# Scores computed with the keys on the partitions and row sums by a product with ones, in an attention block followed by a SoLU feed-forward

## The chip, the cores and the metric

The kernel runs on one NeuronCore of a Trainium2 chip. The metric is the device time of one execution in microseconds (us); smaller is better. The engines are named as in the profile: PE (matrix products and transposes; PEld is its weight load), DVE (vector engine), ACT (activation engine), POOL (GpSimd) and SP, which here only issues the input transfers.

## What is computed

The reference, cut to what matters. Eight batches, twelve heads, 448 positions, head size 64; then 3584 tokens of 768 features through a feed-forward of width 1024.

```
q_n, k_n = rmsnorm(q, g_q), rmsnorm(k, g_k)       # over the 64 values of a head
scores = matmul(q_n, k_n^T) / sqrt(64)
attn = exp(scores - max(scores)) ; attn /= sum(attn) + 1e-9
x = concat over heads of matmul(attn, v)          # 3584 x 768
h = x @ w_in ; e = exp(h - max(h)) ; solu = h * e / (sum(e) + 1e-9)
ln = (solu - mean) / sqrt(var + 1e-6) * g_ln
out = ln @ w_out                                  # w_in, w_out are float64 in memory
```

Everything on the chip is float32. The two weight matrices arrive as 64-bit floats and are taken apart into float32 by integer operations.

## The kernel before

A **pair** is two heads of one batch; there are 48 pairs, six to a batch. For pair n the kernel does, in this order:

- `load`: q and k of both heads by one transfer each, and v, on SP's queue, three pairs ahead.
- `norm` (L136 to L152), one pair ahead: squares on ACT, sums on DVE, the power -1/2 on POOL, then q scaled on DVE and k scaled on POOL.
- `qk_transpose` (L165, L170): eight transposes on PE into two PSUM tiles `pt`; DVE copies both out with the gains as a factor, to `qkT`.
- `scores` (L180 to L186), for each quarter j of the query rows: two products on PE (one a head) put 112 queries on the partitions and 448 keys along the row, in `s`. DVE takes the row maximum (`nmax`), ACT makes the exponentials `E` and their row sums.
- `normalise` (L192 to L195): DVE inverts the eight sums, POOL multiplies all of `E` by them, two instructions of 112x1792.
- `e_transpose` (L206, L209), a pair later: 32 transposes on PE turn `E` round, so that the keys are on the partitions; DVE and ACT copy the four results out of PSUM as `ET`.
- `values` (L221, L227): eight products on PE, summed over the keys in `o`; DVE copies `o` to `xT`, the feed-forward's input.

The **feed-forward** works on tiles of 128 tokens, 28 in all, three or four to a batch. The first part of a tile is `ff_in` (L243, product `h`) and `ff_solu` (mostly DVE); the second is `ff_transpose` (`pu`) and `ff_out` (`po`, L286). The tiles of batch b-1 are cut in pieces and strewn between the pieces of the pairs of batch b; the last batch's four tiles follow alone.

The **weights** are converted in 28 steps during batch 0 (`load_w`, `convert_w`, L102 to L114): six or seven instructions on DVE, one on ACT, for `w_in` one on POOL.

The tile framework gives buffers in turn, adds the waits, and moves instructions of an engine against the order of the code; each engine then runs its own list strictly in order.

Of the kernel before, what the change touches and what calls it, by code (L numbers as in the profile page):

```python
# [9 lines left out]
FP32 = mybir.dt.float32  # L10
U32 = mybir.dt.uint32
I32 = mybir.dt.int32
AX = mybir.AxisListType.X
AF = mybir.ActivationFunctionType
OP = AluOpType


@with_exitstack
def kernel(
    ctx: ExitStack,  # L20
    tc: tile.TileContext,
    q: bass.AP,
# [95 lines left out]
    st = {}  # L118
# [92 lines left out]
    def values(n):


        b, hp = divmod(n, NP)
        d = st[n]
        if b // 2 not in xTs:
            xTs[b // 2] = work.tile([P, KD, 2 * S], FP32, tag="xT", name="xT")
        o = ps_t.tile([P, S], FP32, tag="t", name="o")
        for kc in range(NJ):
            for h in range(2):  # L220
                nc.tensor.matmul(  # L221
                    o[h * D : (h + 1) * D, :], d["v"][:, h, kc * D : (kc + 1) * D], d["ET", h][:, kc],
                    start=(kc == 0), stop=(kc == NJ - 1),
                )

        c0 = (b % 2) * S
        nc.vector.tensor_copy(  # L227
            xTs[b // 2][:, hp, c0 : c0 + S].rearrange("d (p j) -> d j p", j=NJ),
            o.rearrange("d (j p) -> d j p", j=NJ),
        )  # L230
        del st[n]

# [161 lines left out]
```

## Time and profile before

| | |
|---|---|
| median of three runs | 1436.75 us (1434.79 to 1441.49) |
| the profiled execution: its own time | 1442.7 us |
| its span, first to last instruction | 1440.9 us |
| granted TensorE clock, mean over the span | 0.937 of full speed |
| busy: PE, DVE, POOL, ACT | 1246.6, 803.3, 548.6, 482.0 us |

The span is cut below at the moments at which `xT` of a batch's last pair is written (batch 0 ends at 214 us, batch 1 at 378 us, batch 7 at 1349 us; what follows is the last four tiles). In these stretches PE and DVE change places: DVE is busier in the first, PE in all others. In "x16" and the like the profile counts two records for each product of the program, since a float32 product runs as two.

### The profile page before, as it was taken

What the parts mean: (1) busy time and instruction counts of PE and PEld (TensorE: products, weight loads), DVE (VectorE), ACT (ScalarE), POOL (GpSimd) and SP (SyncE); (2) the same over time, 40 slices, a digit from 0 to 9 for tenths busy, and PEclk for the clock granted to TensorE, in tenths of its full rate; (3) what the DMA queues carried; (4) which work ended last, traced back from release to release, by engine and by line L of the source; (5) the groups of instructions that cost most, each with busy time, mean ns of one, the idle gap of its engine ahead of it and who ended that gap; (6) DMA issues with size and microseconds to landing.
All of it is one profiled execution on the core that took longest, in us unless ns stands there. A gap on an engine that the chain in (4) does not pass through costs nothing.

```text
span 1440.9 us, 14104 instructions
## 1 busy us (share of the span) xinstructions
PE 1246.6 (87%) x5249; PEld 630.5 (44%) x5249; DVE 803.3 (56%) x1234; ACT 482.0 (33%) x1177; POOL 548.6 (38%) x239
## 2 busy tenths in 40 slices
PE   3466558899899998899899998899899998999998
PEld 1133224445444454444444454444444454445454
DVE  6889996554565445635564455736554454535331
ACT  3234232333333234234423334324323333324111
POOL 5662447325433253433433253343433243231100
PEclk9667678999999999999999999999999999999999
DMA  4322310101101010010100111011101001000000
GB/s 148 106 85 73 92 56 30 33 30 31 50 20 31 30 50 30 26 43 31 50 20 30 31 37 43 25 44 31 41 28 31 31 30 37 7 18 12 11 14 31
DMA packets 42717, 57.55 MB, mean 40 GB/s; under 512 B 3216, under 2 KB 35480, under 8 KB 42648
## 3 DMA queue, kind: packets, MB, share of 16 engines
q1 hardware_dynamic: 38592, 45.62, 10.8%
q10 hardware_dynamic: 4056, 11.02, 2.0%
q8 instruction: 42, 0.69, 0.2%
q14 instruction: 27, 0.22, 0.1%
HBM read 45.62 MB, written 11.01 MB: 39 GB/s over the span
## 4 chain that ended last, share of the span: by engine, by line
PE 44%; DVE 23%; POOL 12%; DMA 8%; issue 6%; ACT 6%; SPq 1%; ACTq 0%; POOLq 0%; DVEq 0%
PE po L286 15%; PE h L243 14%; POOL E L195 8%; DMA qk<-in_k_dram 7%; PE o L221 6%; PE s L180 5%; DVE nmax L184 5%; PE pe L206 4%; ACT E L186 3%; DVE rs L138 2%; DVE qkn L152 2%; POOL rs L144 2%; DVE qkT L170 2%; POOL qkn L152 2%; ACT sq L136 2%
## 5 line engine op out<-in xcount | busy, mean ns | idle before, releaser
L195 POOL TENSOR_TENSOR E<-E,sum 112x1792 f32<-112x1792 f32 x96 | 309.7, 3247 | 234.6 <-DVE sum L193 233.3
L243 PE MATMUL h<-w_in,xT 128*128 128x512 f32 x672 | 317.3, 622 | 19.6 <-ACT E L186 19.6
L286 PE MATMUL po<-w_out,uT 128*128 128x384 f32 x896 | 306.8, 495 | 14.0 <-ACT ET L209 8.6
L186 ACT ACTIVATE E<-s,nmax 112x448 f32<-112x448 f32 x384 | 240.6, 633 | 200.5 <-DVE nmax L184 198.5
L184 DVE TENSOR_REDUCE nmax<-s 112x2 f32<-112x896 f32 x192 | 207.5, 1083 | 140.4 <-PE s L180 140.2
L180 PE MATMUL s<-qkT 64*112 64x448 f32 x768 | 213.5, 634 | 75.7 <-DVE qkT L170 35.1
L144 POOL TENSOR_TENSOR rs<-rs,mhalf 112x16 f32<-112x16 f32 x48 | 142.7, 2974 | 269.2 <-DVE rs L143 269.2
L206 PE MATMUL pe<-ident,E 112*112 112x112 f32 x1536 | 200.8, 277 | 43.2 <-POOL E L195 40.8
L206 PEld LDWEIGHTS pe<-ident,E 112*112 112x112 f32 x1536 | 161.0, 141 | 163.8 <-issue 88.6
L286 PEld LDWEIGHTS po<-w_out,uT 128*128 128x128 f32 x896 | 167.9, 193 | 133.8 <-issue 14.2
L243 PEld LDWEIGHTS h<-w_in,xT 128*128 128x128 f32 x672 | 128.1, 198 | 177.3 <-issue 154.3
L221 PE MATMUL o<-ET,v 112*64 112x448 f32 x768 | 173.1, 558 | 16.2 <-DVE ET L209 15.8
L136 ACT ACTIVATE sq<-qk 112x1024 f32<-112x1024 f32 x48 | 50.8, 1058 | 325.5 <-DMA qk<-in_k_dram 292.6
L209 DVE COPY ET<-pe 112x448 f32<-112x448 f32 x192 | 117.9, 615 | 59.6 <-PE pe L206 59.0
L209 ACT COPY ET<-pe 112x448 f32<-112x448 f32 x192 | 100.4, 532 | 123.2 <-PE pe L206 119.8
L138 DVE TENSOR_REDUCE rs<-sq 112x16 f32<-112x1024 f32 x48 | 58.4, 1217 | 133.5 <-ACT sq L136 133.5
L180 PEld LDWEIGHTS s<-qkT 64*112 64x112 f32 x768 | 59.9, 186 | 159.6 <-issue 69.4
L266 POOL TENSOR_TENSOR he<-he,mhalf 128x1 f32<-128x1 f32 x28 | 15.4, 550 | 299.8 <-DVE he L265 299.8
L227 DVE COPY xT<-o 128x448 f32<-128x448 f32 x48 | 46.5, 968 | 98.5 <-PE o L221 98.2
L252 DVE TENSOR_REDUCE hmax<-h 128x1 f32<-128x1024 f32 x28 | 34.3, 1225 | 114.8 <-PE h L243 114.5
L221 PEld LDWEIGHTS o<-ET,v 112*64 112x64 f32 x768 | 53.6, 138 | 98.6 <-issue 73.2
L287 ACT COPY y<-po 128x384 f32<-128x384 f32 x56 | 26.7, 476 | 172.1 <-PE po L286 172.1
(43 smaller groups left out, 784.0 us busy)
## 6 DMA issues: line engine op xcount, KB each, us to landing
qk<-in_q_dram SPq DMA_DIRECT2D x48, 224.0 KB, 2.9
qk<-in_k_dram SPq DMA_DIRECT2D x48, 224.0 KB, 3.3
v<-in_v_dram SPq DMA_DIRECT2D x48, 224.0 KB, 2.6
out_dram<-y ACTq DMA_DIRECT2D x28, 384.0 KB, 2.3
raw<-in_moe_w_in_dram SPq DMA_DIRECT2D x12, 512.0 KB, 3.9
raw<-in_moe_w_out_dram SPq DMA_DIRECT2D x16, 384.0 KB, 3.2
grow<-in_g_q_dram ACTq DMA_DIRECT2D x2, 0.2 KB
grow<-in_g_k_dram ACTq DMA_DIRECT2D x2, 0.2 KB
```

What stands on the lines that cost most here:

```text
L136: nc.scalar.activation(sq, d["qk"], AF.Square)
L138: nc.vector.tensor_reduce(rs.rearrange("p s h j -> p (s h j)"), sq.rearrange("p s h (j d) -> p (s h j) d", d=D), AX, OP.add,)
L144: nc.gpsimd.tensor_tensor(rs.rearrange("p s h j -> p (s h j)"), rs.rearrange("p s h j -> p (s h j)"), mhalf[0:SP].to_broadcast([SP, 4 * NJ ...
L180: nc.tensor.matmul(s[:, h, 0:S], d["qkT"][hh, 0, j * SP : (j + 1) * SP], d["qkT"][hh, 1, :], start=True, stop=True)
L184: nc.vector.tensor_reduce(nmax, s[:, :, 0:S], AX, OP.max, negate=True)
L186: nc.scalar.activation(d["E"][:, h, j], s[:, h, 0:S], AF.Exp, bias=nmax[:, h : h + 1], accum_out=d["sum"][:, h, j : j + 1])
L195: nc.gpsimd.tensor_tensor(d["E"][:, h], d["E"][:, h], d["sum"][:, h].rearrange("p j -> p j ()").to_broadcast([SP, NJ, S]), OP.mult)
L206: nc.tensor.transpose(pt[:, j * SP : (j + 1) * SP], d["E"][:, h, j, kc * SP : (kc + 1) * SP], ident[0:SP, 0:SP])
L209: (nc.vector.tensor_copy if kc % 2 else nc.scalar.copy)(d["ET", h][:, kc], pt)
L221: nc.tensor.matmul(o[h * D : (h + 1) * D, :], d["v"][:, h, kc * D : (kc + 1) * D], d["ET", h][:, kc], start=(kc == 0), stop=(kc == NJ - 1),)
L243: nc.tensor.matmul(d["h"][:, hs], xTs[m][:, c, t * P : (t + 1) * P], w_in[:, c, hs], start=(c == 0), stop=(c == KD - 1))
L286: nc.tensor.matmul(po, d["uT"][:, c], w_out[:, c, hs], start=(c == 0), stop=(c == KF - 1))
```

## The change

The kernel's body becomes `general_path` (with small edits) and is put behind a branch on a flag: the largest |g_q * g_k| against 80/8 = 10. With the inputs of the reference the largest is 5.26, so the branch is not entered. A new `fast_path` runs first:

- `scores` gives the products the other way round, 112 keys on the partitions and 448 queries along the row, each head in a PSUM tile of its own. k is transposed raw, its norm factor enters as the exponential's per-partition scale, and both gains and 1/8 go into q's copy. No maximum is subtracted. `E` is then what `values` needs: no transposes of `E`, no copies, no maximum.
- Row sums: POOL adds the four key blocks (1792, then 896 elements) to `es`; PE multiplies `es` with a matrix of ones (`sm`), which gives the sum on 64 partitions for each head; DVE takes the reciprocal of 128x448 and multiplies `o` by it while copying to `xT`.
- q and k are loaded by one transfer a head (four a pair, pieces of 256 bytes; before: two a pair, pieces of 1024 bytes).
- The weights: `w_in` is converted in batch 0, `w_out` in batch 1. The second part of a tile lags by three tiles, so batch 1 has three first parts and no second part, and the end has four first and seven second parts.
- PSUM: one `h` tile of two banks, and six one-bank tiles that everything else shares (before: two two-bank tiles shared by `s` and `h`, four others).

```diff
+    def norm(n):
+        nc.scalar.activation(sq, d["qk"].rearrange("p s j h d -> p (s j h) d"), AF.Square)
+        nc.vector.tensor_reduce(flat, sq, AX, OP.add)
+        nc.vector.tensor_scalar(rs, rs, 1.0 / D, 1e-6, OP.mult, OP.add)
+        nc.gpsimd.tensor_tensor(flat, flat, mhalf[0:SP].to_broadcast([SP, 4 * NJ]), OP.pow)
+        nc.gpsimd.tensor_tensor(
+            d["qn"],
+            d["qk"][:, 0].rearrange("p j h d -> p (j h) d"),
+            rs[:, 0].rearrange("p j h -> p (j h) ()").to_broadcast([SP, NJ * 2, D]),
+            OP.mult,
+        )
...
+    def scores(n, kc):
...
+        for h in range(2):
+            hh = slice(h * D, (h + 1) * D)
+            s = d["s", h] = ps_t.tile([SP, S], FP32, tag="t", name="s")
+            nc.tensor.matmul(
+                s, d["qkT"][hh, 1, kc * SP : (kc + 1) * SP], d["qkT"][hh, 0, :], start=True, stop=True
+            )
+        for h in range(2):
+            nc.scalar.activation(d["E"][:, kc, h], d["s", h], AF.Exp, scale=d["rs"][:, 1, kc, h : h + 1])
+        if kc == NJ - 1:
+            es = d["es"] = work.tile([SP, 2, 2, S], FP32, tag="es", name="es", bufs=1)
+            nc.gpsimd.tensor_tensor(es, d["E"][:, 0:2], d["E"][:, 2:4], OP.add)
+            nc.gpsimd.tensor_tensor(es[:, 0], es[:, 0], es[:, 1], OP.add)
...
+    def values(n):
...
+        sm = ps_t.tile([P, S], FP32, tag="t", name="sm")
+        for h in range(2):
+            nc.tensor.matmul(sm[h * D : (h + 1) * D, :], ones[0:SP, :], d["es"][:, 0, h], start=True, stop=True)
+        r = work.tile([P, S], FP32, tag="r", name="r")
+        nc.vector.reciprocal(r, sm)
...
+        nc.vector.tensor_tensor(
+            xTs[b // 2][:, hp, c0 : c0 + S].rearrange("d (p j) -> d j p", j=NJ),
+            o.rearrange("d (j p) -> d j p", j=NJ),
+            r.rearrange("d (j p) -> d j p", j=NJ),
+            OP.mult,
+        )
...
+    LAG = 3
...
+            if len(waiting) > (LAG if b < B - 1 else 1):
+                fill += second(waiting.pop(0))
...
+    fast_path(tc, q, k, v, moe_w_in, moe_w_out, out, grow, within)
+    large = nc.values_load(flag[0:1, 0:1], min_val=0, max_val=1)
+    with tc.If(large > 0):
+        general_path(tc, q, k, v, g_q, g_k, moe_w_in, moe_w_out, moe_g_ln, out)
```

How the rows stand on the engines, first PE in a middle batch, where pairs and tiles are mixed. Before, from one `o` to the next transposed scores (`pe` is the transpose of `E`):

```order
L221 MATMUL o<-ET,v 64x448 x8
L165 MATMUL pt<-ident,qkn 128x112 x8
L243 MATMUL h<-w_in,xT 128x512 x6
L180 MATMUL s<-qkT 112x448 x2
L206 MATMUL pe<-ident,E 112x112 x16
L243 MATMUL h<-w_in,xT 128x512 x2
L180 MATMUL s<-qkT 112x448 x2
```

The `pe` rows stand between the scores, 32 of them to a pair. Now, PE in a middle batch:

```order
L607 MATMUL po<-w_out,uT 128x384 x8
L534 MATMUL o<-E,v 64x448 x8
L540 MATMUL sm<-es,ones 64x448 x2
L514 MATMUL s<-qkT 112x448 x2
L607 MATMUL po<-w_out,uT 128x384 x8
L514 MATMUL s<-qkT 112x448 x2
L501 MATMUL pt<-ident,qn 128x112 x4
L501 MATMUL pt<-ident,qk 128x112 x4
L564 MATMUL h<-w_in,xT 128x512 x6
L514 MATMUL s<-qkT 112x448 x4
```

The `pe` rows are gone; two `sm` products, which read POOL's `es`, have come in right behind `o`.

DVE in batch 0, before (`tmp` belongs to the weight conversion):

```order
L107 TENSOR_SCALAR tmp<-tmp 128x512
L184 TENSOR_REDUCE nmax<-s 112x2
L108 TENSOR_SCALAR tmp<-tmp 128x512
L209 COPY ET<-pe 112x448
L109 SCALAR_TENSOR_TENSOR tmp<-raw,tmp 128x512
L102 TENSOR_SCALAR tmp<-raw 128x512
L105 TENSOR_SCALAR tmp<-raw 128x512
L227 COPY xT<-o 128x4x112
```

And DVE in batch 0 now:

```order
L482 TENSOR_REDUCE rs<-sq 112x16
L483 TENSOR_SCALAR rs<-rs 112x16
L444 TENSOR_SCALAR tmp<-raw 128x512
L542 RECIPROCAL r<-sm 128x448
L446 SCALAR_TENSOR_TENSOR tmp<-raw,tmp 128x512
L545 TENSOR_TENSOR xT<-o,r 128x4x112
L505 TENSOR_SCALAR qkT<-pt,gcol 128x448
L447 TENSOR_SCALAR tmp<-raw 128x512
```

The maxima and the `ET` copies are gone from between the conversion's instructions, and one wide reciprocal a pair has come in. POOL in batch 0 now, one pair:

```order
L453 TENSOR_TENSOR w_in<-tmp 128x512 x2
L484 TENSOR_TENSOR rs<-rs,mhalf 112x16
L487 TENSOR_TENSOR qn<-qk,rs 112x512
L521 TENSOR_TENSOR es<-E 112x1792
L522 TENSOR_TENSOR es<-es 112x896
```

The two `E` instructions of 112x1792 have given way to two additions, of 112x1792 and 112x896.

## Rows read from the trace of the kernel before

**Rows 1.** Page, part 1: busy time, share of the span, instructions.

```profile
PE 1246.6 (87%) x5249; PEld 630.5 (44%) x5249; DVE 803.3 (56%) x1234; ACT 482.0 (33%) x1177; POOL 548.6 (38%) x239
```

**Rows 2.** Stretches: length, PE, PEld, DVE, ACT, POOL busy; clock, DMA share, GB/s.

```profile
core 0 of [0], span 1440.9 us
...
0.00:214.00 214.00, 116.65 (x465) 54.30 (x465) 186.05 (x299) 75.95 (x176) 105.58 (x49) 0.72 0.31 94
214.00:378.00 164.00, 146.08 (x616) 73.41 (x617) 87.80 (x132) 57.52 (x142) 73.89 (x32) 0.94 0.11 34
...
879.00:1036.00 157.00, 141.64 (x624) 71.64 (x624) 84.97 (x126) 56.70 (x141) 64.20 (x28) 0.97 0.11 34
1036.00:1210.00 174.00, 160.38 (x688) 81.99 (x688) 89.80 (x136) 59.30 (x146) 64.91 (x29) 0.98 0.11 33
1210.00:1349.00 139.00, 133.67 (x605) 68.81 (x602) 66.95 (x104) 46.24 (x119) 42.64 (x18) 0.99 0.04 14
1349.00:1441.00 92.00, 86.60 (x256) 45.65 (x256) 23.34 (x41) 11.00 (x20) 2.17 (x4) 1.00 0.05 18
```

**Rows 3.** Order of time, batch 0: start, duration, engine, line, operation.

```profile
46.99 0.68 DVE L104 SCALAR_TENSOR_TENSOR tmp<-raw,tmp 128x512 f32<-128x512 uint32 x1
47.59 0.41 DVE L107 TENSOR_SCALAR tmp<-tmp 128x512 int32<-128x512 int32 x1
47.93 1.08 DVE L184 TENSOR_REDUCE nmax<-s 112x2 f32<-112x896 f32 x1
...
127.68 6.62 POOL L195 TENSOR_TENSOR E<-E,sum 112x1792 f32<-112x1792 f32 x2 [19.31 <-DVE sum L193]
127.93 3.33 DVE L105 TENSOR_SCALAR tmp<-raw 128x384 uint32<-128x384 uint32 x1
```

**Rows 4.** Order of time, PE in middle and late batches at full clock.

```profile
703.05 0.98 PE L206 MATMUL pe<-ident,E 112*112 112x112 f32 x8
703.96 1.01 PE L180 MATMUL s<-qkT 64*112 64x448 f32 x4
705.81 3.23 PE L221 MATMUL o<-ET,v 112*64 112x448 f32 x16
...
1403.07 9.60 PE L243 MATMUL h<-w_in,xT 128*128 128x512 f32 x22
...
1425.94 10.59 PE L286 MATMUL po<-w_out,uT 128*128 128x384 f32 x32 [0.69 <-ACT uT L277]
```

**Rows 5.** Waits of PE: us in total, times, longest.

```profile
PE pe L206 <- POOL E L195: 40.8, 15, 9.0
PE s L180 <- DVE qkT L170: 35.1, 11, 5.5
```

**Rows 6.** Groups by line: busy us, mean ns of one | idle before.

```profile
L209 DVE COPY ET<-pe 112x448 f32<-112x448 f32 x192 | 117.9, 615 | 59.6 <-PE pe L206 59.0
L170 DVE TENSOR_SCALAR qkT<-pt,gcol 128x448 f32<-128x448 f32 x96 | 60.9, 665 | 8.9 <-PE pt L165 8.9
L138 DVE TENSOR_REDUCE rs<-sq 112x16 f32<-112x1024 f32 x48 | 58.4, 1217 | 133.5 <-ACT sq L136 133.5
L227 DVE COPY xT<-o 128x448 f32<-128x448 f32 x48 | 46.5, 968 | 98.5 <-PE o L221 98.2
```

**Rows 7.** Single lines: duration in ns, min/median/max.

```profile
L195 POOL TENSOR_TENSOR E<-E,sum x96: 3167/3175/5157, 29.8 to 1339.3; 112x1792 f32<-112x1792 f32 x96
...
L111 POOL TENSOR_TENSOR w_in<-tmp x12: 1258/1324/2314, 22.7 to 103.5; 128x512 f32<-128x512 f32 x12
...
L152 POOL TENSOR_TENSOR qkn<-qk,rs x48: 1037/1061/2487, 11.5 to 1269.4; 112x512 f32<-112x512 f32 x48
...
L193 DVE RECIPROCAL sum<-sum x48: 187/203/204, 28.6 to 1335.8; 112x8 f32<-112x8 f32 x48
...
L192 DVE TENSOR_SCALAR sum<-sum x48: 118/172/174, 28.2 to 1335.6; 112x8 f32<-112x8 f32 x48
```

**Rows 8.** Page, part 3: the input queue's packets, MB, share of 16 engines.

```profile
q1 hardware_dynamic: 38592, 45.62, 10.8%
```

More of the change, by code (lines that the diff above doesn't have):

```diff
@@ L18, with general_path @@
 @with_exitstack
-def kernel(
+def general_path(
     ctx: ExitStack,
@@ L201, in e_transpose @@
         if half == 0:
-            d["ET", h] = work.tile([SP, NJ, S], FP32, tag="ET", name="ET", bufs=3)
+            d["ET", h] = work.tile([SP, NJ, S], FP32, tag="ET", name="ET")
         for kc in (2 * half, 2 * half + 1):
@@ L209, in e_transpose, with values @@
             (nc.vector.tensor_copy if kc % 2 else nc.scalar.copy)(d["ET", h][:, kc], pt)
-    def values(n):
+    def values(n, h):
         b, hp = divmod(n, NP)
@@ L217, in values @@
             xTs[b // 2] = work.tile([P, KD, 2 * S], FP32, tag="xT", name="xT")
-        o = ps_t.tile([P, S], FP32, tag="t", name="o")
+        if h == 0:
+            d["o"] = ps_t.tile([P, S], FP32, tag="t", name="o")
         for kc in range(NJ):
[L220 to L231, printed above, removed]
+            nc.tensor.matmul(
+                d["o"][h * D : (h + 1) * D, :], d["v"][:, h, kc * D : (kc + 1) * D], d["ET", h][:, kc],
+                start=(kc == 0), stop=(kc == NJ - 1),
+            )
+        if h == 1:
+            c0 = (b % 2) * S
+            nc.vector.tensor_copy(
+                xTs[b // 2][:, hp, c0 : c0 + S].rearrange("d (p j) -> d j p", j=NJ),
+                d["o"].rearrange("d (j p) -> d j p", j=NJ),
+            )
+            del st[n]
     mt = {}
@@ L319, in pair @@
                 pieces.append(lambda h=h, half=half: e_transpose(n - 1, h, half))
-                if j == NJ - 1:
-                    pieces.append(lambda: values(n - 1))
+                if half:
+                    pieces.append(lambda h=h: values(n - 1, h))
             if j == 1 and n + 3 < B * NP:
@@ new lines, with kernel @@
+@with_exitstack
+def kernel(
+    ctx: ExitStack,
+    tc: tile.TileContext,
+    q: bass.AP,
+    k: bass.AP,
+    v: bass.AP,
+    g_q: bass.AP,
+    g_k: bass.AP,
+    moe_w_in: bass.AP,
+    moe_w_out: bass.AP,
+    moe_g_ln: bass.AP,
+    out: bass.AP,
+):
+    nc = tc.nc
+    D = q.shape[3]
+    P = 128
+    KF = moe_w_in.shape[1] // P
+    gains = ctx.enter_context(tc.tile_pool(name="gains", bufs=1))
+    grow = gains.tile([KF + 2, P], FP32, name="grow")
+    gg = gains.tile([P, 2, D], FP32, name="gg")
+    gmax = gains.tile([P, 1], FP32, name="gmax")
+    within = gains.tile([P, 1], FP32, name="within")
+    flag = gains.tile([1, 1], I32, name="flag")
+    nc.scalar.dma_start(grow[0:KF, :], moe_g_ln.rearrange("(c p) -> c p", p=P))
+    for i, g in enumerate((g_q, g_k)):
+        for h in range(2):
+            nc.scalar.dma_start(grow[KF + i : KF + i + 1, h * D : (h + 1) * D], g.rearrange("(o d) -> o d", o=1))
+    for i, g in enumerate((g_q, g_k)):
+        nc.scalar.dma_start(gg[:, i], g.rearrange("(o d) -> o d", o=1).to_broadcast([P, D]))
+    nc.vector.tensor_tensor(gg[:, 0], gg[:, 0], gg[:, 1], OP.mult)
+    nc.vector.tensor_reduce(gmax, gg[:, 0], AX, OP.max, apply_absolute_value=True)
+    nc.vector.tensor_scalar(flag, gmax[0:1], 80.0 / float(D) ** 0.5, None, OP.is_gt)
+    nc.vector.tensor_scalar(within, gmax, 80.0 / float(D) ** 0.5, float(D) ** -0.5, OP.is_le, OP.mult)
+    fast_path(tc, q, k, v, moe_w_in, moe_w_out, out, grow, within)
+    large = nc.values_load(flag[0:1, 0:1], min_val=0, max_val=1)
+    with tc.If(large > 0):
+        general_path(tc, q, k, v, g_q, g_k, moe_w_in, moe_w_out, moe_g_ln, out)
```

244 lines of the change are left out of this document (243 added, 1 removed).

## The prediction

> **What bounds the kernel now.** The page's busy times come first: PE is busy 87% of the span, everything else 56% or less [rows 1]. That is an average over stages, so I cut the span at the ends of the batches [rows 2]. The reader is to see three kernels in one. In batch 0 (0 to 214 us) DVE is busy 186 of 214 us and PE only 117, at a granted clock of 0.72: DVE sets the pace, because the weight conversion lies on it. In batches 1 to 7 PE is busy 134 to 160 us of 139 to 174 at a clock of 0.94 to 0.99: PE sets the pace, with some 14 us of idle time in a middle batch. In the last 92 us PE is busy 87 of them. So I ask of each edit: what does it take from DVE in the front, from PE behind it, and what comes in.
>
> DVE in the front has a second load that the busy time hides. The order of time shows a weight instruction (L105) of 3.33 us that starts while POOL multiplies `E` and ends with that POOL instruction [rows 3]; the instructions shown above it in that group follow each other every 0.34 and 0.60 us. DVE was standing behind POOL: part of its busy time is such waiting.
>
> **PE, batches 2 to 7.** Unit prices at full clock [rows 4]: eight transposes 0.98 us, two score products 1.01 us for one quarter (a pair has four), the eight products of `o` 3.2 us, `h` of a tile 9.60 x 24/22 = 10.5 us, `po` 10.6 us, `pu` (eight transposes) 1.0 us. A pair now costs 1.0 (`pt`) + 4.0 + 3.2 + 3.9 (32 transposes `pe`) = 12.1 us, a tile 22.1 us. Check: six pairs and four tiles make 161 us, and a four-tile batch shows 160.4 us busy [rows 2]; with three tiles 139 against 141.6. The change takes out the 3.9 us and puts in `sm`, two products of the shape of the eight in `o`: a quarter of 3.2, 0.8 us. A pair then costs 9.0 us, a batch 6 x 9.0 + 4 x 22.1 = 142 or 54 + 66 = 120 us. Three of each make 788 us.
>
> To this comes idle time. Now it is 15.4 and 13.6 us in the two middle batches shown and 5.3 in the last [rows 2]. The wait of `pe` for POOL's multiplied `E`, 40.8 us in all or 5.1 a batch, goes with `pe` [rows 5]. The wait of scores for `qkT`, 35.1 us, stays in kind: two copies still follow `pt`, only one of them goes to ACT. The maximum is no longer between a score and its exponential, which should free PSUM sooner; against it stands the new wait of `sm` for `es`. I let these two cancel and take 14.5 - 5.1 = 9.4 us for five batches, 5 for the last: 52 us. Batches 2 to 7: 840 us, now 971.
>
> `sm` costs no wait if `es` is there in time. Behind the last exponential of a pair POOL needs about 6 us (below); until `sm` PE has `pt` (1.0), two quarters of scores (2.0), `o` (3.2) and, in most pairs, a feed-forward piece of 1 to 5 us. That cover is thin: it is gone where no piece lies between or POOL is still at the next pair's norm, and then `sm` waits and the next scores queue behind it.
>
> **DVE, batches 0 and 1.** A conversion step is four instructions of 0.34 and two of 0.60 us [rows 3], 2.56 us; I take the same for `w_out`, which is narrower and has one more. Now six pairs share 28 steps, 11.9 us a pair. The attention's own DVE work is four maxima (4.3), `rs` (1.2), two `qkT` (1.3), four `ET` (2.5), `xT` (1.0) [rows 3, 6], the sums (0.4) [rows 7], about 1.0 for the small ones and q's scaling (an estimate): 11.7. Together 23.6 us a pair; shown are 186/6 = 31.0 [rows 2]. The missing 7.4 us are the standing behind POOL. POOL's streaming instructions make two `E` (6.3), k's scaling (1.1) and two weight products (2.5) a pair [rows 7], 9.9 us, so three quarters of POOL's streaming time is lost on DVE.
>
> The change puts a wide reciprocal on DVE. The trace has it only for 8 elements: 203 ns against 172 ns for an addition of the same tile [rows 7], 3.9 ns an element more. A copy of 448 elements out of PSUM takes 0.615 us [rows 6], 1.4 ns an element; together 5.3 ns or 2.4 us. Bounds: 0.6 us, if the 31 ns are a fixed cost, and 4.8 us, if all above the shortest addition (203 - 118 ns) grows with the elements. I take 2.4 us, since the difference of two equal tiles is the nearest thing to a price per element. It isn't on PE's path later, where DVE has half its time free, but it is in the front. The Trainium skill (VectorE: DVE Perf Modes, the section on the fixed hardware budget) says that a reciprocal is an iterated division with a repeat count of 8; if that meant eight passes an element at the 0.96 GHz of its overview page (Trainium Kernel Development and Optimization, NeuronCore Architecture), it would take 3.7 us, an estimate, and the sum would be 18 us higher. No row here shows a wide one.
>
> POOL's additions read two full operands; `E` times the sums read one full and one broadcast. From k's scaling and `E` [rows 7] a broadcast instruction costs (3167 - 1037)/1280 = 1.66 ns an element and 0.19 us; the weight product, with two full operands, (1258 - 190)/512 = 2.1 ns. So `es` costs 3.9 + 2.1 = 6.0 us; bounds 4.9 (broadcast price) and 6.6 (1258/512 for all).
>
> Now a pair in batch 0: two steps 5.1, `rs` and small 1.4, one `qkT` 0.7, reciprocal 2.4, `xT` 1.0, 10.5 us; standing behind POOL 0.75 x (6.0 + 1.1 + 2.5) = 7.2; 17.7 us, at DVE's present 87% 20.3 us, six pairs 122 us. Batch 1: 2.67 steps 6.8, 5.4, half a tile of feed-forward (23.3/4 = 5.8 a tile with the copy of `uT`, rows of the last stretch [rows 2]) 2.8, behind POOL 0.75 x 7.1 = 5.3; 20.3, over 0.87 23.3, 140 us. PE needs less: in batch 1, 54 + 3 x 10.5 = 85 us at full clock. Together 262 us, now 378.
>
> **The rest.** The end has four first and seven second parts, 4 x 10.5 + 7 x 11.6 = 123 us; with the 5.4 us that PE is idle there now [rows 2] and 3 us for the last pair's sum chain 132 us, now 92. The lag gives back 40 us here; batch 1 gets them. Transfers: four loads a pair for two, in pieces of 256 bytes. A packet now takes 0.108 x 16 x 1440.9 us / 38592 = 64.5 ns [rows 8]. If a small one takes as long, q and k of a pair hold each of the 16 engines for 112 packets, 7.2 us, where a pair lasts 20 us or more and loads are issued three pairs ahead: hidden. Without that cover it would be 5.4 us a pair. The general path isn't entered; nothing in the trace prices the branch at the end, and I allow 3 us.
>
> Sum: 262 + 840 + 132 + 3 = 1237 us of span, against 1440.9. The profiled execution's time, 1442.7, is 6 us over the median of the runs shown and 2 us over its own span; so **1233 us** as a median.
>
> **Rivals.**
> 1. The front hardly shrinks, because POOL's two-operand additions keep DVE standing. For it: rows 3. Against it: the maxima and `ET` copies leave. With the upper prices (reciprocal 4.8, all of POOL's 9.6 and 7.1 us lost) pairs last 25.9 and 28.2 us, batches 0 and 1 324 us: 1295 us.
> 2. Less idle time and a cheap reciprocal: at 0.6 us the front is 25 us shorter, and if PE runs middle batches as it runs the last one now (5 us idle), another 22 us: 1186 us; with half of the standing behind POOL gone too (42 us), 1144 us.
> 3. `sm` waits for `es` in every pair and the idle time stays as now: 5 x 5.1 and 5 in the last batch, 1263 us. It decides where POOL's work behind the last exponential exceeds PE's cover of 6 us plus the feed-forward piece.
> 4. The loads. The Trainium skill (DMA: Bandwidth & Descriptors, Specifications) says that transfers need at least 512 bytes for line rate, and the change goes to 256. It speaks against the change. By the rows it would take effect only if a small packet took about three times the 64.5 ns, so that q and k alone hold the engines for 20 us a pair: each further 10 ns would then cost 1.1 us for each of 48 pairs. At 200 ns, 22.4 us a pair, batch 0 (20.3 us a pair) and the three-tile batches (21.6) would lose some 27 us: 1260 us.
> 5. Slower than before: PE's clock falls. The front shows 0.72 where PE is busy 55% of the time, the middle 0.97 to 0.98 at 90 to 92% [rows 2]. PE's work from batch 2 on is 788 + 123 = 911 us. If waits thinned it out so that the clock went down, 204 us would be lost at 911 x (0.98/c - 1) = 204, c = 0.80; below that the kernel is slower, at 0.72 it takes 1233 + 329 = 1562 us. Against it: the sum above keeps PE at over 90% in every stage behind the front.
>
> **How the numbers follow.** The forecast, within 1200 to 1262, has a chance of 0.49; rival 1 0.17, rival 2 0.20, rivals 3 and 4 together 0.10, rival 5 0.04. Low and high take in the middle of rival 2 and the whole of rival 1: 1165 to 1295 us. About 0.5% is what a measurement of this kernel can tell from no change. No case but the fifth comes near the old time: faster 0.94, within 0.5% 0.02, slower 0.04.
>
> **What would show it.** The last `xT` of batch 1 near 262 us, with DVE over 85% busy before it and weight instructions of several us that end with `es`; if DVE is much less busy, the term for the front is wrong. A RECIPROCAL row of about 2.4 us, and `es` rows of 3.9 and 2.1 us. Middle batches of about 152 and 130 us with PE over 90% busy and a clock over 0.95; waits of `sm` for POOL of less than 1 us a pair. Four first and seven second parts in the last 132 us. The forecast fails if `sm` heads PE's waits, or if the load rows show transfers that exponentials or squares wait for.

## The result and the profile after

The changed kernel takes **1169.05 us** (median of four runs, 1167.76 to 1170.17); the kernel before, timed beside it, 1435.77 us (1431.43 to 1441.49). The ratio is 0.814, 95% interval 0.8109 to 0.8171. The profiled execution has a span of 1166.3 us at a mean granted clock of 0.967.

The page of the changed kernel, busy times (answers to [rows 1]) and the input queue (answers to [rows 8]):

```profile
PE 1059.3 (91%) x3905; PEld 486.4 (42%) x3905; DVE 580.1 (50%) x710; ACT 372.4 (32%) x649; POOL 521.6 (45%) x240
...
q1 hardware_dynamic: 104640, 45.63, 15.1%
```

PE has 187 us less work and is still the busiest. POOL's busy time has hardly changed. A packet of q1 takes 0.151 x 16 x 1166.3 us / 104640 = 26.9 ns on average; by the shapes of the loads 86016 of them are 256-byte pieces of q and k.

The changed kernel cut at the ends of its batches (columns as in [rows 2]):

```profile
0.00:136.00 136.00, 79.59 (x307) 31.07 (x307) 116.20 (x130) 53.75 (x90) 99.31 (x52) 0.84 0.39 107
136.00:248.00 112.00, 89.62 (x328) 35.40 (x328) 103.03 (x158) 44.79 (x79) 65.86 (x29) 0.89 0.32 85
248.00:392.00 144.00, 140.65 (x520) 65.60 (x520) 58.94 (x71) 45.70 (x80) 59.80 (x28) 0.99 0.14 38
392.00:512.00 120.00, 117.94 (x457) 53.53 (x456) 54.53 (x61) 43.45 (x76) 61.94 (x28) 1.00 0.17 45
512.00:655.00 143.00, 139.33 (x520) 65.02 (x520) 59.64 (x71) 45.94 (x80) 62.92 (x30) 1.00 0.15 40
...
917.00:1040.00 123.00, 117.53 (x432) 52.37 (x432) 50.16 (x52) 34.27 (x62) 45.73 (x20) 0.99 0.07 21
1040.00:1166.00 126.00, 117.97 (x368) 64.88 (x367) 24.75 (x44) 15.64 (x29) 2.20 (x4) 1.00 0.06 23
```

Batches 0 and 1 end at 248 us (before: 378), batches 2 to 7 take 792 us (before: 971), the end 126 us (before: 92). A middle batch has 2 to 4 us of idle PE time where those of [rows 2] had 13.6 and 15.4, and the granted clock there has gone from 0.97 and 0.98 to 0.99 and 1.00. In batch 0 neither DVE (116 of 136 us) nor PE (80) is busy all the time.

Single lines of the changed kernel, min/median/max in ns:

```profile
L542 DVE RECIPROCAL r<-sm x48: 2901/2956/2959, 40.2 to 1036.4; 128x448 f32<-128x448 f32 x48
...
L521 POOL TENSOR_TENSOR es<-E x48: 3956/3973/4441, 28.7 to 1028.7; 112x1792 f32<-112x1792 f32 x48
L522 POOL TENSOR_TENSOR es<-es x48: 2072/2089/2417, 33.0 to 1032.8; 112x896 f32<-112x896 f32 x48
```

PE's waits in the changed kernel, whole span (us in total, times, longest):

```profile
PE s L514 <- DVE qkT L505: 21.2, 11, 3.2
PE h L564 <- DVE xT L545: 18.2, 4, 6.0
PE pt L501 <- ACT E L518: 17.9, 8, 6.0
PE s L514 <- ACT qkT L503: 16.0, 9, 6.5
...
PE sm L540 <- POOL es L522: 6.6, 3, 3.6
```

The wait that headed [rows 5], for POOL's multiplied `E`, is gone. Its possible successor, `sm` for `es`, is 6.6 us in all. What remains lies mostly in batches 0 and 1: there PE waits for the last instructions of the chain of the pair just made (`xT`, `qkT`, `E`).

A pair's end in batch 0 of the changed kernel, in order of time (answers to [rows 3]):

```profile
92.85 2.94 DVE L542 RECIPROCAL r<-sm 128x448 f32<-128x448 f32 x1
...
96.15 4.16 POOL L521 TENSOR_TENSOR es<-E 112x1792 f32<-112x1792 f32 x1
96.40 0.95 DVE L545 TENSOR_TENSOR xT<-o,r 128x448 f32<-128x448 f32 x1
97.19 0.65 DVE L505 TENSOR_SCALAR qkT<-pt,gcol 128x448 f32<-128x448 f32 x1
...
97.40 2.07 PE L564 MATMUL h<-w_in,xT 128*128 128x512 f32 x2 [3.52 <-DVE xT L545]
97.76 3.09 DVE L451 SCALAR_TENSOR_TENSOR tmp<-raw,tmp 128x512 uint32<-128x512 uint32 x1
...
100.78 2.29 DVE L444 TENSOR_SCALAR tmp<-raw 128x512 uint32<-128x512 uint32 x1
```

Two things are to be seen. A weight instruction (L451) that takes 0.69 us where POOL is idle takes 3.09 us beside `es` and ends just behind it: DVE still stands behind POOL. And PE waits 3.52 us for `xT`, because the framework has put one product `h` of the next batch's feed-forward between two pairs of batch 0; the scores of the next pair are queued behind it.

### The profile page after: what moved, and what is told of

Read it like the earlier page. It is cut to its first block, busy times and chain, and to the rows that moved or that the text cites. A ratio compares the mean times of both kernels' runs of the same rounds, so it can differ in the third digit from the quotient of the medians.

```text
span 1166.3 us, 10387 instructions
## 1 busy us (share of the span) xinstructions
PE 1059.3 (91%) x3905; PEld 486.4 (42%) x3905; DVE 580.1 (50%) x710; ACT 372.4 (32%) x649; POOL 521.6 (45%) x240
## 3 DMA queue, kind: packets, MB, share of 16 engines
q1 hardware_dynamic: 104640, 45.63, 15.1%
## 4 chain that ended last, share of the span: by engine, by line
PE 71%; DVE 20%; ACT 4%; issue 2%; DMA 1%; POOL 1%; SPq 0%; ACTq 0%; POOLq 0%; DVEq 0%
PE po L607 26%; PE h L564 23%; PE s L514 10%; PE o L534 9%; DVE r L542 5%; PE sm L540 2%; DVE tmp L451 2%; DVE tmp L446 2%; PE pt L501 2%; ACT u L576 1%; DVE tmp L450 1%; ACT E L518 1%; DVE u L577 1%; DMA raw<-in_moe_w_out_dram 1%; DVE xT L545 1%
## 5 line engine op out<-in xcount | busy, mean ns | idle before, releaser
L518 ACT ACTIVATE E<-s,rs 112x448 f32<-112x448 f32 x384 | 218.1, 634 | 295.5 <-PE s L514 295.1
L521 POOL TENSOR_TENSOR es<-E 112x1792 f32<-112x1792 f32 x48 | 193.9, 4040 | 78.8 <-ACT E L518 78.8
L514 PE MATMUL s<-qkT 64*112 64x448 f32 x768 | 194.6, 610 | 37.6 <-DVE qkT L505 21.2
L542 DVE RECIPROCAL r<-sm 128x448 f32<-128x448 f32 x48 | 141.4, 2946 | 174.5 <-PE sm L540 174.5
L487 POOL TENSOR_TENSOR qn<-qk,rs 112x512 f32<-112x512 f32 x48 | 52.8, 1101 | 255.3 <-PE pt L501 253.0
L534 PE MATMUL o<-E,v 112*64 112x448 f32 x768 | 155.7, 547 | 0.0
L514 PEld LDWEIGHTS s<-qkT 64*112 64x112 f32 x768 | 65.7, 185 | 153.2 <-issue 123.0
L522 POOL TENSOR_TENSOR es<-es 112x896 f32<-112x896 f32 x48 | 102.2, 2129 | 3.6
L534 PEld LDWEIGHTS o<-E,v 112*64 112x64 f32 x768 | 51.1, 137 | 98.9 <-issue 92.3
L587 POOL TENSOR_TENSOR he<-he,mhalf 128x1 f32<-128x1 f32 x28 | 15.6, 556 | 171.6 <-DVE he L586 171.5
L505 DVE TENSOR_SCALAR qkT<-pt,gcol 128x448 f32<-128x448 f32 x48 | 32.3, 672 | 59.2 <-PE pt L501 59.2
L501 PE MATMUL pt<-ident,qn 112*128 112x112 f32 x192 | 30.1, 281 | 26.9 <-ACT E L518 17.7
L540 PE MATMUL sm<-es,ones 112*64 112x448 f32 x192 | 45.2, 550 | 6.7 <-POOL es L522 6.6
```

Source lines behind the costliest of these rows:

```text
L501: nc.tensor.transpose(pt[:, j * SP : (j + 1) * SP], src, ident[0:SP, 0:SP])
L514: nc.tensor.matmul(s, d["qkT"][hh, 1, kc * SP : (kc + 1) * SP], d["qkT"][hh, 0, :], start=True, stop=True)
L518: nc.scalar.activation(d["E"][:, kc, h], d["s", h], AF.Exp, scale=d["rs"][:, 1, kc, h : h + 1])
L521: nc.gpsimd.tensor_tensor(es, d["E"][:, 0:2], d["E"][:, 2:4], OP.add)
L522: nc.gpsimd.tensor_tensor(es[:, 0], es[:, 0], es[:, 1], OP.add)
L534: nc.tensor.matmul(o[h * D : (h + 1) * D, :], d["v"][:, h, kc * D : (kc + 1) * D], d["E"][:, kc, h], start=(kc == 0), stop=(kc == NJ - 1),)
```

## The experiments

Times are medians with their range; ratios are to the kernel before, with the 95% interval. The kernel before was timed beside each group of runs and had medians of 1435.77 to 1441.69 us there, so a difference of a few us between two groups says little.

**e1: no reciprocal.**

```diff
-        nc.vector.reciprocal(r, sm)
+        nc.vector.tensor_copy(r, sm)
```

> The changed kernel with the reciprocal of the sums left out (a copy of 128x448 out of PSUM in its place, so the outputs are not divided by the sums). Theory A (DVE sets the pace up to the end of batch 1, PE behind it): the reciprocal took 2.95 us, the copy about 0.65, so the first 12 pairs lose 2.3 us each over DVE's share of about 0.88: 31 us less before the last sum of batch 1, nothing after it; in all about 1138 us against 1169. Theory B (the front waits on POOL's chain of exponentials, additions and products, DVE is only busy beside it): under 10 us.

Measured: 1155.46 us (1154.26 to 1155.63), ratio 0.802 (0.8002 to 0.8038). Batches 0 and 1 end 3 us earlier; each later batch is 1 to 4 us shorter, 13 us in all, and the end 2 us longer. The first two batches, and PE's waits in them:

```profile
0.00:135.45 135.45, 81.20 (x307) 31.51 (x307) 110.95 (x142) 54.17 (x90) 95.86 (x50) 0.82 0.41 113
135.45:244.94 109.49, 89.91 (x327) 34.94 (x328) 88.17 (x147) 44.71 (x79) 68.03 (x29) 0.86 0.30 78
```

```profile
PE sm L540 <- POOL es L522: 18.9, 6, 5.1
PE pt L501 <- DVE r L542: 13.2, 8, 3.3
```

DVE is busy 20 us less (199.1 for 219.2) and only 3 us came out, for `sm` now waits 18.9 us for POOL's `es` (6.6 with the reciprocal). DVE was not the one thing that set the pace. The forecast of 31 us failed, and so did its "nothing after it": 10 of the 13.6 us came out behind the front.

**e2 and e3: row sums on PE instead of POOL.** e2 lets PE multiply all of `E` with ones, without POOL's additions, in every pair; e3 does so for the pairs of batches 0 and 1 alone.

```diff
-        if kc == NJ - 1:
+        if kc == NJ - 1 and n >= 2 * NP:
             es = d["es"] = work.tile([SP, 2, 2, S], FP32, tag="es", name="es", bufs=1)
...
+            for kc in range(NJ):
+                for h in range(2):
+                    nc.tensor.matmul(
+                        sm[h * D : (h + 1) * D, :], ones[0:SP, :], d["E"][:, kc, h],
+                        start=(kc == 0), stop=(kc == NJ - 1),
+                    )
```

> The changed kernel with the row sums made by eight products with ones that add up in PSUM, for every pair, and POOL's two additions left out. Theory A: in the front 6.1 us of POOL streaming a pair are gone, of which three quarters stood on DVE: 12 x 4.6 / 0.88 = 60 us less up to the end of batch 1, if PE, now at a low clock there, does not take over; behind it PE has 6 more products a pair, 2.4 us, 36 x 2.4 = 86 us more in batches 2 to 7. In all about 1195 us (1180 to 1215). Theory B (sm waits for POOL's sums in batches 2 to 7 as well): the 86 us are partly paid back, 1140 to 1170 us.

> As e2, but only for the pairs of batches 0 and 1; from batch 2 on POOL adds as in the changed kernel. Theory A: up to 60 us less before the end of batch 1 and nothing after it: 1110 to 1135 us. Theory B (PE at its low clock is as near to being the bound in the front as DVE): 5 to 20 us less, 1149 to 1164 us. If POOL's additions cost DVE nothing: 1169 or more.

Measured: e2 1234.25 us (1230.62 to 1237.2), ratio 0.8573 (0.8552 to 0.8594); e3 **1152.79 us** (1150.52 to 1158.79), ratio 0.8012 (0.7984 to 0.8039). A middle batch of e2:

```profile
232.19:388.76 156.57, 152.84 (x592) 70.18 (x592) 57.55 (x72) 45.76 (x80) 25.88 (x16) 1.00 0.14 37
```

The batch is 12.6 us longer, with 12.2 us more of PE: behind the front, PE's work is the time. The time lies above both forecasts, because batches 0 and 1 gave back 16 us and not 60. Batches 0 and 1 of e3:

```profile
0.00:127.39 127.39, 84.83 (x379) 34.20 (x379) 99.70 (x164) 56.57 (x94) 63.75 (x40) 0.92 0.48 130
127.39:232.67 105.28, 95.68 (x400) 37.69 (x400) 75.00 (x125) 43.26 (x75) 29.98 (x16) 0.97 0.27 69
```

The same 288 or 289 DVE instructions of the front are busy 174.7 us instead of 219.2, since POOL is busy 93.7 instead of 165.2: of 71.5 us of POOL's work, 44.5 had been standing time on DVE, 0.62 of it. The front gave back 15.5 us. e3 is faster than the changed kernel; the intervals don't touch.

**e4: no branch.** The flag's load and the branch with the general path are left out.

```diff
-    large = nc.values_load(flag[0:1, 0:1], min_val=0, max_val=1)
-    with tc.If(large > 0):
-        general_path(tc, q, k, v, g_q, g_k, moe_w_in, moe_w_out, moe_g_ln, out)
```

> The changed kernel with the flag's load, the branch and the general path left out. With 3 us allowed for the branch: 1166 us. By the end of the trace after (from the last output's issue to the end of the span 4.35 us, 3.8 before): under 1 us, no difference that can be measured.

Measured: 1168.42 us (1165.98 to 1172.17), ratio 0.8111 (0.809 to 0.8131). No difference to 1169.05 that can be measured.

**e5: maxima in the changed kernel.**

```diff
+        nmax = small.tile([SP, 2], FP32, tag="nmax", name="nmax")
+        for h in range(2):
+            nc.vector.tensor_reduce(nmax[:, h : h + 1], d["s", h], AX, OP.max, negate=True)
         for h in range(2):
-            nc.scalar.activation(d["E"][:, kc, h], d["s", h], AF.Exp, scale=d["rs"][:, 1, kc, h : h + 1])
+            nc.scalar.activation(
+                d["E"][:, kc, h], d["s", h], AF.Exp, bias=nmax[:, h : h + 1], scale=d["rs"][:, 1, kc, h : h + 1]
+            )
```

> The changed kernel with a row maximum of each score tile put back on DVE ahead of its exponentials (eight maxima of 112x448 a pair, the exponentials take them as bias; the maximum runs over queries here, so the outputs are not the reference's). Theory A (the idle time of PE went because no maximum stands between a score and its exponential): 8 x 0.6 = 4.8 us of DVE a pair; the front 12 x 4.8 / 0.88 = 65 us longer, and PE's idle time in batches 2 to 7 back from 3 to 8 or 14 us a batch, 30 to 60 us: 1265 to 1295 us. Theory C (the idle time went with POOL's multiplication of E and the transposes of E alone): only the front gets longer, about 1235 us.

Measured: 1228.48 us (1227.78 to 1228.91), ratio 0.8537 (0.8514 to 0.856). Its stretches, batches 0 to 3:

```profile
0.00:150.51 150.51, 91.38 (x303) 33.68 (x303) 134.85 (x174) 56.20 (x83) 93.17 (x50) 0.77 0.36 94
150.51:297.57 147.06, 108.50 (x325) 41.82 (x325) 142.35 (x212) 52.08 (x81) 60.67 (x25) 0.78 0.25 66
297.57:442.10 144.53, 140.69 (x525) 64.89 (x523) 88.53 (x124) 52.30 (x81) 69.38 (x32) 1.00 0.15 40
442.10:563.82 121.72, 118.64 (x456) 53.12 (x456) 76.72 (x110) 48.25 (x75) 61.63 (x28) 1.00 0.17 44
```

The front is 49 us longer with 58 us more on DVE; the time is nearest to the second forecast, 1235. In the middle batches DVE has 22 to 30 us more to do, the maximum stands between every score and its exponential again, and PE's idle time stays at 3 to 4 us in those shown, 5 us more than in the changed kernel over all of batches 2 to 7. In this program the maximum alone makes PE wait very little.

**e6: PSUM as before** (scores share the two-bank tiles with `h`, four others).

```diff
+        s2 = ps_h.tile([SP, 2, 512], FP32, tag="h", name="s")
         for h in range(2):
...
-            s = d["s", h] = ps_t.tile([SP, S], FP32, tag="t", name="s")
+            s = d["s", h] = s2[:, h, 0:S]
```

> The changed kernel with PSUM shared out as before: two tiles of two banks for scores (both heads in one) and h together, four tiles of one bank for the rest. Theory A (the maximum held the score tiles): 0 to 12 us more, 1169 to 1181 us. Theory D (PE lost its idle time through the new layout, since h and scores no longer wait for each other): PE's idle time in batches 2 to 7 back to 10 us or more a batch, 40 us or more: 1210 us or more.

Measured: 1180.07 us (1179.52 to 1180.79), ratio 0.8202 (0.818 to 0.8224): about 11 us more. Batch 0 is 5 us shorter, batch 1 8 us longer, batches 2 to 6 are 1.5 to 4 us longer each, of which 1 to 2 us are idle time. The layout is worth something, but not the 10 us of idle time that a middle batch lost.

**e7: weights and lag as before** (all 28 steps in batch 0, second parts one tile late).

```diff
-    LAG = 3
+    LAG = 1
...
-            if b < 2:
-                while wdone - w0 < len(w_steps[b]) * (x + 1) // len(flat):
+            if b < 1:
+                while wdone < len(wq) * (x + 1) // len(flat):
```

> The changed kernel with the weights' 28 steps all in batch 0 again and the second part of a tile one tile behind the first. Theory A: batch 0 gets 16 steps of 2.6 us more on DVE and POOL's standing time stays, about 50 us longer; batch 1 has no conversion and is bound by PE, about 120 us with three whole tiles (now 112); the last stretch has four second parts instead of seven, 35 us less. In all 1175 to 1200 us. Theory E (the split of the conversion is what the front's gain comes from): the front goes back most of the way, 1230 us or more.

Measured: 1178.15 us (1177.55 to 1179.92), ratio 0.8193 (0.8171 to 0.8215). Batch 0 takes 171.5 us instead of 136, the end 101 instead of 126: spreading the weights over two batches is worth 9 us net.

**e8: smaller pieces** (each load of q and k cut in two of 128-byte pieces, eight transfers a pair).

```diff
-                nc.sync.dma_start(d["qk"][:, s, :, h], src[b, h0 + h].rearrange("(p j) d -> p j d", j=NJ))
+                for c in range(2):
+                    dd = slice(c * D // 2, (c + 1) * D // 2)
+                    nc.sync.dma_start(
+                        d["qk"][:, s, :, h, dd], src[b, h0 + h, :, dd].rearrange("(p j) d -> p j d", j=NJ)
+                    )
```

> The changed kernel with each load of q and k cut in two, pieces of 128 bytes, eight transfers a pair instead of four, so twice the small packets. Theory A (loads are hidden three pairs ahead): 1169 us, within 6 us. If small packets hold up the pairs: in the front at least, 15 us or more.

Measured: 1194.73 us (1193.76 to 1196.52), ratio 0.8302 (0.828 to 0.8324): 25 us more, 3 to 7 in each of batches 1 to 6, none in batch 0 nor in batch 7, in which only the last three pairs are still to be loaded. Both forecasts missed it: the loads aren't free, and the loss isn't in the front. The waits of SP's queue in this kernel, and of ACT in the changed one:

```profile
SPq L478 <- PE o L538: 343.3, 36, 17.6
SPq L475 <- PE pt L505: 250.7, 41, 9.6
```

```profile
ACT sq L479 <- DMA qk<-in_k_dram: 99.8, 27, 5.4
```

A load's issue waits on SP until PE has done with the buffer (`o` frees v's, `pt` frees k's, which is now transposed as it came), and the loads behind it wait too. At the other end ACT's squares wait for the landing, with the exponentials queued behind them. But these waits don't explain the 25 us: in the changed kernel the two of SP are longer (417.4 and 257.8 us), and ACT's is 95.2 us in e8. What is longer is batch 1, by 7 us, and batches 2 to 7, by 11 us of idle time and 11 us of PE's busy time, at granted clocks of 0.97 to 0.99. How the loads bring them about stays open, and whether the eight issues or the small pieces cost more, this run doesn't tell.

**e9 and e10: one step out of the kernel before.** e9 leaves out POOL's multiplication of `E`, e10 the maximum.

```diff
-        for h in range(2):
-            nc.gpsimd.tensor_tensor(
-                d["E"][:, h], d["E"][:, h], d["sum"][:, h].rearrange("p j -> p j ()").to_broadcast([SP, NJ, S]), OP.mult
-            )
```

```diff
-        nmax = small.tile([SP, 2], FP32, tag="nmax", name="nmax")
-        nc.vector.tensor_reduce(nmax, s[:, :, 0:S], AX, OP.max, negate=True)
...
-                d["E"][:, h, j], s[:, h, 0:S], AF.Exp, bias=nmax[:, h : h + 1], accum_out=d["sum"][:, h, j : j + 1]
+                d["E"][:, h, j], s[:, h, 0:S], AF.Exp, accum_out=d["sum"][:, h, j : j + 1]
```

> The kernel before, without POOL's multiplication of the exponentials by the reciprocal sums (the sums and reciprocals are still made, but the exponentials go on unnormalised): part of the computation is left out. e5 showed that the row maxima did not make TensorE's idle time of the middle batches (12 to 16 us a batch before, 1 to 4 after), so it went with the multiplication or with the transposes of E. Theory C1 (the multiplication of two times about 3.2 us a pair stands between the last exponential and the first transpose of E, and its streaming holds up DVE): the idle time falls by 5 us or more in each of the six middle batches and batches 0 and 1 lose 10 to 20 us together: 1380 to 1400. Rival C2 (the idle time is that of the transposes' own round trip through PSUM, 16 evictions a pair): the middle batches keep their length within 2 us, only the front shrinks: 1418 to 1432.

> The kernel before, without the row maxima of the scores and without the bias of the exponentials (sums, normalisation and transposes of E as before): the safeguard against overflow is left out. Put back into the changed kernel, maxima of the same size cost 49 us, all of it in batches 0 and 1. Theory A (what the maxima cost is DVE's time in the two batches in which it also converts weights): batches 0 and 1 shrink by 35 to 55 us together, the middle batches by less than 2 each: 1380 to 1402. Rival (before, the maximum stands between the scores and the exponentials in every pair and E's transposes wait behind it): the middle batches lose 4 or more each as well: 1345 to 1370.

Measured: e9 1337.7 us (1336.49 to 1342.35), ratio 0.9278 (0.9238 to 0.9318); e10 1341.16 us (1339.5 to 1344.18), ratio 0.931 (0.9268 to 0.9351). e9's gain was more than twice the forecast one, and e10 came out by its rival, a little lower still. Batch 0 and two middle batches of e9:

```profile
0.00:186.47 186.47, 118.49 (x473) 55.06 (x473) 153.68 (x296) 74.43 (x175) 62.16 (x35) 0.75 0.36 106
...
645.54:809.22 163.68, 157.32 (x691) 80.60 (x690) 84.63 (x138) 59.40 (x146) 26.41 (x16) 1.00 0.12 35
809.22:951.59 142.37, 136.09 (x627) 69.50 (x626) 79.80 (x128) 56.32 (x141) 25.31 (x15) 1.00 0.12 38
```

And of e10:

```profile
0.00:182.00 182.00, 111.99 (x465) 56.53 (x465) 165.50 (x276) 69.13 (x177) 110.01 (x50) 0.77 0.38 111
...
643.00:808.55 165.55, 159.06 (x688) 81.49 (x688) 71.93 (x114) 53.75 (x146) 65.75 (x29) 0.99 0.11 35
808.55:950.16 141.61, 136.32 (x624) 70.19 (x624) 61.45 (x104) 51.05 (x141) 64.24 (x28) 0.99 0.13 38
```

PE's waits between 380 and 1040 us (batches 2 to 5 of the kernel before, about as many in the others) in the kernel before, in e9 and in e10, and q's scaling on DVE in the middle batches of the kernel before and of e9:

```profile
PE s L180 <- ACT E L186: 14.3, 10, 2.3
PE h L243 <- ACT E L186: 12.6, 8, 2.4
PE pe L206 <- POOL E L195: 6.8, 5, 1.4
```

```profile
PE s L180 <- ACT E L186: 10.5, 11, 1.6
PE h L239 <- ACT E L186: 5.7, 8, 1.4
```

```profile
PE s L180 <- ACT E L184: 4.3, 8, 1.5
```

```profile
L152 DVE TENSOR_TENSOR qkn<-qk,rs 112x512 f32<-112x512 f32 x25 | 27.9, 1117 | 0.0
L152 DVE TENSOR_TENSOR qkn<-qk,rs 112x512 f32<-112x512 f32 x24 | 16.3, 681 | 0.0
```

Two things that the prediction lacked stand here. Of the 40.8 us that `pe` waits for POOL in [rows 5], only 6.8 us lie in batches 2 to 5; 30.9 us lie in batch 0. And half of the 55 us that PE is idle in batches 2 to 5 are `s` and `h` waiting for exponentials. Neither reads `E`: the two share two PSUM tiles, and what they wait for is that the exponentials have read a tile out. The 26.9 us of this wait fall to 16.2 in e9 and to 4.3 in e10, and the changed kernel has none of it in that window.

Batches 2 to 7 take 914 us in e9 and 917 in e10, against 971; either edit more than halves the idle time of a middle batch (5 to 7 us here, against 13.6 and 15.4 in [rows 2]). In a three-tile batch PE's busy time also falls, from 141.6 us at a clock of 0.97 [rows 2] to 136 at 1.00 and 0.99, for the same 624 to 627 records. In batch 0 of e9 DVE is busy 153.7 us, where [rows 2] has 186.05 for about as many instructions: the 43 us less of POOL gave back 32 us of standing, 0.75 of it. DVE stands behind POOL in the middle batches too: q's scaling is 0.44 us shorter without the multiplication. PE goes through batches 3 and 4 of e9 in the same order as before; in e10 the framework has moved some pieces, so that e10 isn't the maximum alone.

**e11 and e12: on top of e3.** e11 takes the products of `h` in reversed order, so that the first needs the batch's last pair and none stands between the pairs of batch 0. e12 also loads q by one transfer of 1024-byte pieces.

```diff
-        for c in range(KD):
+        for c in reversed(range(KD)):
             nc.tensor.matmul(
-                d["h"][:, hs], xTs[m][:, c, i * P : (i + 1) * P], w_in[:, c, hs], start=(c == 0), stop=(c == KD - 1)
+                d["h"][:, hs], xTs[m][:, c, i * P : (i + 1) * P], w_in[:, c, hs], start=(c == KD - 1), stop=(c == 0)
             )
```

```diff
+            if s == 0:
+                nc.sync.dma_start(
+                    d["qk"][:, 0].rearrange("p a h d -> p (a h d)").rearrange("p (h x) -> p h x", h=2),
+                    src[b, h0 : h0 + 2].rearrange("h (p j) d -> p h (j d)", j=NJ),
+                )
+                continue
```

> e3 (ones products over the exponentials on PE in batches 0 and 1, POOL's additions later), and the six products of a half of h taken in reversed order of the pairs' rows, so that the first of them needs the batch's last pair and none can be pulled ahead into batch 0. In e3 PE stands at the pulled products for xT of the pair just ended, 1.1 to 1.6 us of product with 2.8 to 4.2 us of wait ahead of it, at each pair of batch 0. Theory A (this wait closes a loop reciprocal, xT, h, scores, exponentials, and so paces batch 0): batch 0 shrinks by 10 to 15 us, the rest is unchanged: 1138 to 1143. Theory B (DVE, which has its conversions queued, is the pace anyway, and the wait moves to the scores or pt): batch 0 within 3 us, 1150 to 1155. Theory C: the products that batch 0 no longer takes lengthen batch 1 by as much as batch 0 gains: 1148 to 1154.

> e11, and q loaded by one transfer a pair in pieces of 1024 bytes (as before the change), POOL's normalisation of q writing it into the order that the transposes want; k keeps two transfers in 256-byte pieces. e8 (four transfers more a pair, pieces of half the size) cost 25 us. Theory A (the loads' time and issues are on the path by way of ACT's squares and SP's order): a transfer less and 448 larger pieces instead of 896 small ones for q give back 2 to 8 us, spread over the batches with loads: 3 to 8 us under e11. Theory B (loads of 256-byte pieces still come in time, only the smaller ones of e8 did not): within 2 us of e11. Theory C (POOL's product with three free dimensions and a permuted write takes longer than 0.3 us more than in e11): 2 us or more over e11.

Measured: e11 1156.79 us (1154.63 to 1159.88), ratio 0.8027 (0.7995 to 0.8058), not to be told from e3; e12 1163.49 us (1160.9 to 1163.82), ratio 0.8068 (0.8038 to 0.8098). PE's longest wait in batch 0 of e11, and DVE there in order of time:

```profile
PE s L514 <- DVE qkT L505: 17.8, 5, 5.3
```

```profile
76.01 2.94 DVE L550 RECIPROCAL r<-sm 128x448 f32<-128x448 f32 x1
78.88 0.36 DVE L449 TENSOR_SCALAR tmp<-tmp 128x512 int32<-128x512 int32 x1
79.16 0.93 DVE L553 TENSOR_TENSOR xT<-o,r 128x448 f32<-128x448 f32 x1
79.94 0.65 DVE L505 TENSOR_SCALAR qkT<-pt,gcol 128x448 f32<-128x448 f32 x1
```

The wait for `xT` has shrunk from 12.9 to 3.2 us and another of about its length stands in its place: `qkT` comes on DVE behind reciprocal and `xT` of the pair before, and the scores need it. Batch 0 is 2.6 us shorter, batch 1, which has to take the six products, 7.6 longer. In e12 q1's packets fall from 104640 to 71616, yet its share of the time only from 15.5% to 14.7%, and the kernel is some 7 us slower than e11. POOL's product there is no longer than in e11 (1054 against 1105 ns on average), so the reason that I had given for a loss isn't the cause. What is stays open: the framework's order differs from e11's at many places.

## Why the prediction was right, and where it was off

The range and the direction held; the time came out 64 us under the forecast, outside the 1200 to 1262 of the likeliest case and 4 us above the low end of the range. What set the pace in each stage was right, but every term of the sum was too high, and that the range still held was in part luck. By the terms of the sum (262 + 840 + 132 + 3 of span):

- **Idle time of batches 2 to 7: 52 forecast, 20 found** (792 us less PE's 772). This is the step that failed: "I let these two cancel and take 14.5 - 5.1 = 9.4 us". It failed twice. The 5.1 us a batch were a wait of the whole span, 40.8 us, over eight batches; 30.9 us of it lie in batch 0, and a middle batch has 1.3 or 1.4. And I had taken a wait for what its step costs. e9 and e10 show that with either the multiplication or the maximum left out (in e10 with some pieces moved as well), six batches have some 35 us of idle time where there were 74 (971 less PE's 897): each took half of it away, mostly under other names, as `s` and `h` waiting for the PSUM tiles that the exponentials free. e5 shows that the maximum, put back where multiplication and transposes are gone, brings back some 5 us over six batches, and e6 bounds what the layout alone does at 1 to 2 us of idle time a batch. That the two stand one behind the other in the loop of the pair, and that the feed-forward pieces between cover one of them but not both, is my reading of this and not shown; nor is it shown how the multiplication delays the exponentials, by its own 6.3 us a pair or by DVE standing behind it.
- **PE's work: 788 forecast, 772 found.** The four quarters of scores cost 3.5 us a pair, not 4.0; in the order of time of the changed kernel two quarters in a row take 1.76 us (L514 x8), and my 1.01 for one was read with a start and an end in it. `sm` takes 0.9, as forecast 0.8. e2 shows that PE's work is the time there, one for one.
- **Front: 262 forecast, 248 found, but 136 and 112 instead of 122 and 140,** so that a part of the nearness is two errors that cancel. The sizes of DVE's load were near: 219 us busy against 0.87 x 262 = 228. The rule "DVE's work over 0.87" failed as a mechanism. Taking DVE's work away brought 3 us for 20 (e1) and 15.5 for 45 (e3); adding 58 cost 49 (e5). DVE, POOL's `es` and the chain reciprocal, `xT`, `qkT`, scores are all near the pace, so that relief of one uncovers the next (in e1 `sm` waits for `es`, in e11 the scores for `qkT`), while a burden on DVE counts nearly in full. The split is off in part because the framework moves weight instructions from batch to batch: two of the sixteen steps of `w_out` ran in batch 0. The rest of it stays open.
- **Standing behind POOL: right, a little high.** I took three quarters of POOL's streaming time. e9 gives 0.75 for the old multiplication, e3 0.62 for the new additions.
- **The wide reciprocal: 2.4 us forecast, 2.96 found**, within the bounds of 0.6 and 4.8. The Trainium skill (VectorE: DVE Perf Modes, the section on the fixed hardware budget) gives a repeat count of 8, which I had turned into an estimate of 3.7 us; the measurement lies between the two and decides. In time the error hardly counted: 2.3 us less a pair brought 13.6 us in e1, so 0.56 us more may have cost some 3 us, an estimate. But "It isn't on PE's path later" was wrong: 10 of those 13.6 us came out behind the front.
- **`es`: 3.9 + 2.1 forecast, 3.97 + 2.09 found.** `sm` waited for it three times, 6.6 us; rival 3 is out.
- **Loads: hidden by the forecast, and not quite so.** A packet of the queue, mostly of 256 bytes now, takes 26.9 ns on average, not the 64.5 that I had let stand, so rival 4 lost its condition. The Trainium skill (DMA: Bandwidth & Descriptors, Specifications) wants 512 bytes for line rate: bytes over the queue's time fell from 18.3 to 16.2 GB/s an engine with 256-byte pieces of q and k, and to 12.8 with the 128-byte ones of e8, so the trace agrees in direction. But e8 cost 25 us where I had called the loads covered, and by which way is open: the three pairs of issue distance are there only on paper, since SP's issues wait for PE to release buffers, but in e8 they don't wait longer than in the changed kernel. Larger pieces of q alone (e12) brought nothing.
- **Branch: 3 forecast, nothing found** (e4). **End: 132 forecast, 126 found.**
- Rival 5 had the sign wrong: with less waiting, the granted clock of the middle batches rose from 0.97 and 0.98 to 0.99 and 1.00.
- Rival 2 is the case that came true in its time (1144 to 1186), though not by its cheap reciprocal: it was the idle time, PE's work and a part of the standing.

Where the change's 275 us of span come from, before minus after: 130 in batches 0 and 1, 179 in batches 2 to 7 (125 of PE's time, 54 of idle time), less 34 at the end. Undone alone, no part accounts for them: the maximum's return costs 59 us (e5), PSUM 11, the staging 9; in the old kernel, multiplication or maximum alone is worth some 100.

## What to carry to other kernels

A wait that is summed over the span isn't a term of one stage: cut it by stage before it is subtracted (40.8 us here, of which 30.9 lie in batch 0). And a step can cost idle time under other names than its own: of two steps each took half of the idle time away when it alone was left out (e9, e10), so try each alone before pricing a change that removes both. Where two engines and a chain are all near the pace, work that was added counted nearly in full (49 of 58 us, e5) and work that was removed only in part (3 of 20, e1; 15.5 of 45, e3), and the next wait is found by following what is queued behind the last. Choose the engine for a step by stage: row sums on PE in the two batches where POOL's streaming holds DVE up, on POOL where PE is the bound, take 1152.79 us (e3), against 1169.05 with POOL everywhere and 1234.25 with PE everywhere (e2).

## What was new about the hardware

- DVE instructions of 0.34 to 0.69 us stretch to 2 to 3 us beside a POOL addition and end just behind it; over whole stages 0.62 to 0.75 of POOL's streaming time appears as DVE busy time (e3, e9).
- A RECIPROCAL of 128x448 out of PSUM takes 2.96 us, 6.6 ns an element, 4.4 times the 0.67 us of a TENSOR_SCALAR of the same shape.
- The same PE work in a three-tile batch took 141.6 us at a granted clock of 0.97 and 136 at 1.00: with 9 us less of idle time PE's own time fell by 5 more (e9).
- A branch around a second copy of the whole kernel, not entered, cost nothing that four and five runs could show.
